# TensorE in program order in the recurrence of a fused three-stage kernel, with whole blocks of 128-row MoE1 matmuls between its steps

## The chip, the cores and the metric

The kernel runs on one core of one Trainium2 chip. The metric is the device time of one execution in microseconds (us); lower is better. A core has a matmul engine (TensorE; PE in the profile, PEld its weight loads), VectorE (DVE), ScalarE (ACT), GpSimd (POOL) and SyncE (SP), which issues all of this kernel's DMAs. Each engine works through its own instructions in the order in which they were written, and semaphores make it wait for the others.

## The reference

Three stages follow one another. The first is a recurrence over 768 time steps for 4 batches of 8 heads of width 40; the second, MoE1, is a dense layer with an ELU; the third, MoE2, mixes 8 experts with weights from an iterated normalisation.

```python
for t in range(S):                                   # recurrence, S = 768
    y[:, :, t] = einsum('bhd,bhde->bhe', r_t, state)
    Sa = einsum('bhde,bhe->bhd', state, a_t)
    state = state * w_t[:, :, None, :] - einsum('bhd,bhe->bhde', Sa, b_t) \
            + einsum('bhd,bhe->bhde', v_t, k_t)
x = y.transpose(0, 2, 1, 3).reshape(3072, 320)
h = x @ w_in                                         # MoE1: 320 -> 2048 -> 320
g = where(h > 0, h, exp(min(h, 0)) - 1)
x = g @ w_out
P = exp(logits - max)                                # MoE2: gate, 8 normalisations, 8 experts
for e in range(8):
    out += P[:, e:e+1] * (maximum(x @ w1[e], 0) @ w2[e])
```

## The kernel before

**Recurrence.** The 768 steps are cut into 24 chunks of 32. A chunk c is worked off in named steps. E1, E2 and E3 build transposes and the masked product `Am`; E3 writes `Am` to DRAM (`Ad`), and SyncE reads it back as `LT`, laid out for a triangular solve. T (`tsolve`, L377 and L384) is that solve: 62 dependent VectorE instructions, whose result goes through DRAM (`Td`) to `TT`. E4 and H1 form the right-hand side in two PSUM banks, ScalarE copies it to `RH`, H2 multiplies it by `TT`, ScalarE writes `VU`, H3 forms the state `Y` (VectorE, L454), GpSimd scales it to `Yw`, H4 transposes `Yw` to `Ss`. O1 (copies `uE`, one on ScalarE and one on VectorE, L401), O2 (masked product `Gm`) and O3 form the output, which VectorE multiplies into `xT` and SyncE stores to `yd` in DRAM. `prep` makes the decay products (two VectorE scans, `F` and `xE`). The steps of a chunk are issued in the order of the string `PLAN["order"]`; `E3+2` means E3 for chunk c+2, `O1+-1` means O1 for chunk c-1. `TT` is so needed by H2 some one and a half chunks after its E3.

**MoE1** goes by 12 blocks of 256 tokens. A block b needs the output of chunks 2b and 2b+1: `xprep` loads the two halves `yt` from `yd` (one buffer), transposes them and splits them into `X`. A block has 16 units. `m1_mm1` is the first half of a unit, eight matmuls into one PSUM tile `ph` (L536), the last with 64 rows; then ScalarE (two `m`, then `gh`), VectorE (`g`, L542) and GpSimd (`gl`) form the activation in two parts. `m1_mm2` is the second half, for the unit two before: eight matmuls (L560 to L568) that add into `a01` and `a2`, the last with 64 columns (L568). Before, `moe1` yields after every matmul; `step` counts the recurrence's own matmuls and calls `madv` after every four of them, with weights from `PLAN["wt"]`.

**Order of instructions.** A scheduler lists each engine's instructions by priority and by its own estimate of times; matmuls of several steps and units may change places on TensorE. Nothing fixes their order but data and buffers.

**MoE2** starts when MoE1 ends: 7,680 matmuls of 512 or 320 columns (L707, L747 to L749).

Of the kernel before, what the change touches and what calls it, by code (L numbers as in the profile page):

```python
# [9 lines left out]
F32 = mybir.dt.float32  # L10
# [90 lines left out]
def build(ctx, tc, r, k, v, w, a, b, w_in, w_out, wg, w1, w2, wa_d, kb_d, re_d, ro_d, vt_d, wp_d, consts, out, C, off):  # L101
# [13 lines left out]
    V, A, G, T, SY = nc.vector, nc.scalar, nc.gpsimd, nc.tensor, nc.sync  # L115

# [51 lines left out]
    # ------------------------------------------------------------ MoE1 weights  # L168
# [40 lines left out]
    # ------------------------------------------------------------ recurrence  # L209
# [101 lines left out]
    def E1(c):  # L311
        z = st[c]
        z.KB = r2.tile([128, 2, H * D], F32, tag="KB", name="KB", bufs=3)
        for u in range(2):
            for g in range(NG):
                T.transpose(PS["E1"][u][:, 128 * g:128 * g + HR], z.KE[0:HR, g, u, :], ident[0:HR, 0:HR])  # L316
                yield
            o, i = unpad(z.KB[:, u, :], PS["E1"][u])
            cp("KB", u, o, i)

    def E2(c):
# [3 lines left out]
        for g in range(NG):  # L325
            T.transpose(PS["E2"][0][:, 128 * g:128 * g + HR], xv[0:HR, g, :], ident[0:HR, 0:HR])
            yield
# [3 lines left out]
    def masked(PS, K, lhs, rhs, dst):  # L331
        for u in range(2):
            for g in range(NG):
                for bi in range(2):
                    x0 = 64 * (NG * u + g)
                    T.matmul(PS[64 * bi:64 * bi + 64, x0:x0 + 64], lhsT=lhs(u, g)[0:K, 64 * bi:64 * bi + 64], rhs=rhs[0:K, g, u, :, C * bi:C * bi + C], start=True, stop=True)  # L336
# [66 lines left out]
    def H1(c):  # L403
# [7 lines left out]
        for j in range(2):  # L411
            for g in range(NG):
                for bb in range(B):
                    T.matmul(PS["H1"][j][C * bb:C * bb + C, D * g:D * g + D], lhsT=z.aE[64 * j:64 * j + D, g, C * bb:C * bb + C], rhs=Ywv[64 * j:64 * j + D, g, bb, :], start=False, stop=True, skip_group_check=True)
                    yield
            cp("RH", j, z.RH[:, HD2 * j:HD2 * j + HD2], PS["H1"][j][:, 0:HD2])

    def H2(c):
        z = st[c]
        for h in range(H):  # L420
            for u in range(2):
                x = h % NG * 2 + h // NG
                T.matmul(PS["H2"][0][64 * u:64 * u + 64, D * x:D * x + D], lhsT=z.TT[64 * u:64 * u + 64, x, :], rhs=z.RH[64 * u:64 * u + 64, D * h:D * h + D], start=True, stop=True)
# [9 lines left out]
    def H3(c):  # L433
# [3 lines left out]
        for bi in range(2):  # L437
            for g in range(NG):
                for u in range(2):
                    for j in range(2):  # L440
# [3 lines left out]
                        T.matmul(PS["H3"][bi][64 * j:64 * j + D, c0:c0 + D], lhsT=z.KB[p0:p0 + 2 * C, u, D * h:D * h + D], rhs=z.VU[p0:p0 + 2 * C, u, D * (2 * g + j):D * (2 * g + j) + D], start=True, stop=True)  # L444
# [11 lines left out]
    def H4(c):  # L456
        if c == 0:
            return
        for i in range(2 * NG):
# [3 lines left out]
            T.transpose(PS["H4"][x][:, 128 * y:128 * y + HR], yw, ident[0:HR, 0:HR])  # L463
# [7 lines left out]
    def O1(c):  # L471
# [14 lines left out]
    def O3(c):  # L486
# [24 lines left out]
    def xprep(blk):  # L511
        X = xtiles[blk] = (late[0] if blk % 2 else mt).tile([128, 6, 256], F32R, tag=f"X{blk % 2}", name="X", bufs=1)
        for t in range(2):
# [6 lines left out]
            for i in range(3):  # L520
                T.transpose(ps[:, 128 * i:128 * i + 128], yt[:, 128 * i:128 * i + 128], ident)
# [7 lines left out]
    ORD1 = ((0, 0, 128), (1, 1, 128), (2, 2, 128), (0, 3, 128), (1, 4, 128), (3, 0, 128), (4, 1, 128), (2, 5, 64))  # L529
# [21 lines left out]
    def m1_mm2(blk, f):  # L551
# [540 lines left out]
```

## Time and profile before

| | |
|---|---|
| time, median of 3 runs | 2424.52 us (2417.68 to 2428.02) |
| span of the profiled execution | 2419.9 us (the profile gives no other time for it) |
| busy in it | PE 94%, DVE 47%, ACT 30%, POOL 20% |
| mean granted TensorE clock | 0.943 |
| first copy to `RH` of chunk 2, 5, 21, 23 | 141.6, 269.9, 881.2, 936.1 us |

The span runs from the first to the last instruction of the one execution that was profiled. A busy PE is not a PE at its peak: ends of matmuls are modelled, and a wait inside a row of matmuls counts as busy. The copies to `RH` stand once in each chunk, right behind H1, and so mark its beat; the stretches below are cut there. A granted clock of 1.00 is 2.4 GHz, 0.50 is 1.2 GHz, and a number between them is a mean over both.

### The profile page before, as it was taken

Reading aid. Unit: us, or ns where it says so; the run is one execution under the profiler, and the core shown is the slowest. Engines: PE = TensorE matmul, PEld = TensorE weight load, DVE = VectorE, ACT = ScalarE, POOL = GpSimd, SP = SyncE. Lnnn points to the kernel's source line nnn. Section 1 sums busy time; section 2 is a strip of 40 time slices with the busy share of each in tenths; the row PEclk is TensorE's granted clock in tenths of the full one; section 3 lists DMA queues with packets and bytes.
Section 4 is the critical chain, followed back from the end, with each engine's and each line's share of the span. In section 5 each row is a group of like instructions: output and inputs, shape, how many; then the busy total and the mean of one; then the engine's idle time right before and its main releaser. Section 6 shows DMA issues by size and latency. Waiting matters only on the chain.

```text
span 2419.9 us, 48157 instructions
## 1 busy us (share of the span) xinstructions
PE 2281.2 (94%) x19908; PEld 2023.0 (84%) x19908; DVE 1127.5 (47%) x2878; ACT 733.8 (30%) x1627; POOL 486.9 (20%) x570
## 2 busy tenths in 40 slices
PE   2479999999999999999999999999999999999998
PEld 2467888888888888889999999999999999999997
DVE  7898677777677874153222222222222222222222
ACT  2344344444434445532311211211212212212111
POOL 6354333333333322500200200200200101001000
PEclk8568888899899999999999999999999999999999
DMA  5343333323233332210100100100100100000000
GB/s 153 109 142 87 94 76 89 87 79 93 70 99 78 81 82 63 82 59 1 49 1 1 49 1 1 49 1 4 46 1 12 37 1 25 24 1 19 12 25 32
DMA packets 171771, 121.67 MB, mean 50 GB/s; under 512 B 103000, under 2 KB 151512, under 8 KB 171544
## 3 DMA queue, kind: packets, MB, share of 16 engines
q1 hardware_dynamic: 171544, 118.52, 17.9%
q8 instruction: 158, 2.59, 0.4%
q14 instruction: 69, 0.57, 0.1%
HBM read 99.99 MB, written 18.48 MB: 49 GB/s over the span
## 4 chain that ended last, share of the span: by engine, by line
PE 79%; DVE 12%; DMA 5%; issue 2%; SPq 1%; POOL 1%; ACT 1%; DVEq 0%; ACTq 0%
PE h L707 29%; PE pa L748 9%; PE pa L749 9%; PE pa L747 9%; PE ph L536 7%; DVE Wk L384 3%; DMA WA<-in_wa 2%; DVE Tt L377 2%; PE a L560 2%; PE a L562 2%; PE a L564 1%; DMA LT<-Ad 1%; DVE F L290 1%; DVE Am L340 1%; PE P L336 1%
## 5 line engine op out<-in xcount | busy, mean ns | idle before, releaser
L707 PE MATMUL h<-X,a 128*128 128x512 f32 x3072 | 776.5, 395 | 0.0
L711 DVE SCALAR_TENSOR_TENSOR hl<-h,hh 128x512 fp32r<-128x512 f32 x384 | 264.8, 690 | 875.6 <-ACT hh L710 875.2
L707 PEld LDWEIGHTS h<-X,a 128*128 128x128 f32 x3072 | 564.5, 188 | 103.5
L710 ACT ACTIVATE hh<-h 128x512 fp32r<-128x512 f32 x384 | 230.2, 600 | 1021.6 <-PE h L707 1018.1
L748 PE MATMUL pa<-a,hl 128*128 128x320 f32 x1536 | 474.7, 310 | 0.0
L747 PE MATMUL pa<-a,hh 128*128 128x320 f32 x1536 | 472.1, 308 | 0.3 <-ACT logits L587 0.3
L749 PE MATMUL pa<-a,hh 128*128 128x320 f32 x1536 | 468.6, 309 | 0.0
L536 PE MATMUL ph<-X,Wt 128*128 128x256 f32 (+1 forms) x1536 | 309.1, 325 | 5.1 <-DVE g L542 5.0
L748 PEld LDWEIGHTS pa<-a,hl 128*128 128x128 f32 x1536 | 288.7, 188 | 16.0
L747 PEld LDWEIGHTS pa<-a,hh 128*128 128x128 f32 x1536 | 288.8, 188 | 14.7 <-ACT logits L587 0.4
L749 PEld LDWEIGHTS pa<-a,hh 128*128 128x128 f32 x1536 | 287.3, 188 | 0.0
L675 POOL TENSOR_TENSOR a<-rw,a 128x384 fp32r<-128x384 f32 x64 | 65.1, 1016 | 1061.8 <-ACT a L673 1048.4
L536 PEld LDWEIGHTS ph<-X,Wt 128*128 128x128 f32 (+1 forms) x1536 | 237.5, 207 | 42.6 <-issue 7.4
L377 DVE TENSOR_TENSOR Tt<-Wk,LT 128x60 f32<-128x60 f32 (+24 forms) x744 | 208.7, 285 | 44.2 <-DMA LT<-Ad 25.9
L384 DVE TENSOR_TENSOR Wk<-Wk,Tt 128x60 f32<-128x60 f32 (+24 forms) x744 | 210.1, 287 | 16.6
L546 POOL TENSOR_TENSOR gl<-g,gh 128x256 fp32r<-128x256 f32 x192 | 145.8, 762 | 278.6 <-ACT gh L544 260.5
L758 DVE SCALAR_TENSOR_TENSOR acc<-pa,Pg,acc 128x320 f32<-128x320 f32 x168 | 84.3, 544 | 114.8 <-PE pa L749 114.8
L542 DVE SCALAR_TENSOR_TENSOR g<-m,ph 128x256 f32<-128x256 f32 x192 | 79.7, 416 | 123.5 <-ACT m L540 120.4
L544 ACT ACTIVATE gh<-g 128x256 fp32r<-128x256 f32 x192 | 79.2, 416 | 158.6 <-DVE g L542 59.6
L539 ACT ACTIVATE m<-ph 128x256 f32<-128x256 f32 x192 | 71.5, 381 | 120.6 <-PE ph L536 119.2
L540 ACT ACTIVATE m<-m 128x256 f32<-128x256 f32 x192 | 78.5, 417 | 4.1
L316 PE MATMUL P<-cst,KE 104*128 104x104 f32 x192 | 32.3, 300 | 46.7 <-DVE Am L340 23.5
(173 smaller groups left out, 2474.0 us busy)
## 6 DMA issues: line engine op xcount, KB each, us to landing
LT<-Ad SPq DMA_DIRECT2D x24, 512.0 KB
rw<-in_moe_w SPq DMA_DIRECT2D x64, 160.0 KB
WA<-in_wa SPq DMA_DIRECT2D x24, 416.0 KB
KE<-in_kb SPq DMA_DIRECT2D x24, 416.0 KB
rw<-in_moe_w SPq DMA_DIRECT2D x64, 128.0 KB
VU<-in_vt SPq DMA_DIRECT2D x24, 320.0 KB
raw<-in_wp SPq DMA_DIRECT2D x16, 384.0 KB
raw<-in_moe_w_out SPq DMA_DIRECT2D x16, 320.0 KB
```

Source lines behind the costliest of these rows:

```text
L377: V.tensor_tensor(out=tv, in0=Wk[:, 0:ni, j:j + 1].to_broadcast([128, ni, nt]), in1=z.LT[:, j, j + 1:C].unsqueeze(1).to_broadcast([128, ni ...
L384: dve["T"] = V.tensor_tensor(out=Wk[:, 0:ni, j + 1:C], in0=Wk[:, 0:ni, j + 1:C], in1=tv, op=ALU.subtract)
L536: T.matmul(ph, lhsT=Wt[0:kp, wi, 128 * f:128 * f + 128], rhs=X[0:kp, xi, :], start=(i == 0), stop=(i == 7))
L542: V.scalar_tensor_tensor(out=g, in0=m, scalar=-1.0, in1=ph, op0=ALU.add, op1=ALU.max)
L546: G.tensor_tensor(out=gl, in0=g, in1=gh.bitcast(F32), op=ALU.subtract)
L707: T.matmul(h, lhsT=a1[:, wi, :], rhs=X[bk][:, xi, :], start=(i == 0), stop=(i == 7))
L710: A.activation(out=hh, in_=h, func=AF.Relu)
L711: V.scalar_tensor_tensor(out=hl, in0=h, scalar=0.0, in1=hh.bitcast(F32), op0=ALU.max, op1=ALU.subtract)
L747: T.matmul(o, lhsT=hh[:, ts_], rhs=a2[:, 0, :], start=(f == 0), stop=False)
L748: T.matmul(o, lhsT=hl[:, ts_], rhs=a2[:, 0, :], start=False, stop=False)
L749: T.matmul(o, lhsT=hh[:, ts_], rhs=a2[:, 1, :], start=False, stop=(f == NF2 - 1))
L758: V.scalar_tensor_tensor(out=at, in0=o, scalar=Pg[:, tt, e:e + 1], in1=at, op0=ALU.mult, op1=ALU.add)
```

## The change

From chunk 2 on TensorE's instructions are issued in program order: every matmul and transpose of the recurrence, of `xprep`, of MoE1 and of the gate is wrapped in `pin`, which keeps it behind the one before. `moe1` yields after half a unit, so that `m+2` in the new order string issues eight matmuls of `m1_mm1` and eight of `m1_mm2` in one piece, and `m+3` three such halves. Nothing is issued inside a step any more. A chunk has 16 halves, 8 units; chunks 2 to 4 have two thirds of that. `xprep` has a place of its own, `x`. The last matmul of each half is widened: L536's eighth from 64 rows to 128 (the added rows of `Wt` meet rows of `X` that are now written too), L568's from 64 columns to 128.

```diff
-    "order": "E4 O1+-1 H1 ld+3 lu+1 m+8 O2+-1 m+4 O3+-1 H2 prep+2 H3 E3+2 T+2 E1+2 E2+2 H4 m+4 lv w",
+    "order": "E4 H1 m+2 O1+-1 H2 m+3 O2+-1 H3 m+3 ld+3 lu+1 prep+2 O3+-1 m+2 H4 E3+2 T+2 m+2 E1+2 m+2 x E2+2 m+2 lv w",
...
+    def pin(ins):
+        return tc.keep_in_program_order(ins) if chain["on"] else ins
...
-            V.tensor_tensor(out=X[0:64, 5, sl], in0=pv[0:64, 2, :], in1=X[0:64, 2, sl].bitcast(F32), op=ALU.subtract)
+            V.tensor_tensor(out=X[:, 5, sl], in0=pv[:, 2, :], in1=X[:, 2, sl].bitcast(F32), op=ALU.subtract)
...
-    ORD1 = (..., (4, 1, 128), (2, 5, 64))
+    ORD1 = (..., (4, 1, 128), (2, 5, 128))
...
-            T.matmul(ph, lhsT=Wt[0:kp, wi, 128 * f:128 * f + 128], rhs=X[0:kp, xi, :], start=(i == 0), stop=(i == 7))
-            yield
+            pin(T.matmul(ph, lhsT=Wt[0:kp, wi, 128 * f:128 * f + 128], rhs=X[0:kp, xi, :], start=(i == 0), stop=(i == 7)))
...
-        T.matmul(a2[0:64], lhsT=Wo(f)[:, 256:320], rhs=gl, start=False, stop=e, skip_group_check=True)
-        yield
+        pin(T.matmul(a2, lhsT=Wo(f)[:, 256:384], rhs=gl, start=False, stop=e, skip_group_check=True))
...
-                yield from m1_mm1(*units[i])
+                m1_mm1(*units[i])
+                yield
             if i >= LAG:
-                yield from m1_mm2(*units[i - LAG])
+                m1_mm2(*units[i - LAG])
...
+        chain["on"] = True
+        acc = 0
+        for c in range(2, NCH + 1):
             for n, o in order:
...
                 elif n == "m":
-                    madv(o)
+                    acc += o * (2 if c < 5 else 3)
+                    madv(acc // 3)
+                    acc %= 3
+                elif n == "x":
+                    try_xprep()
```

How the order moves is shown at two places; the lines of the changed kernel lie two higher in the recurrence (L414 is now L416) and one lower at the end of a unit.

First TensorE, H1 in a chunk of the middle. Before, its 32 matmuls (`P<-Yw,aE`; the profile lists each of them as two) stand in pieces between matmuls of MoE1 (`a<-gh`, `a<-gl`):

```order
L414 MATMUL P_99<-Yw,aE 32x40 x10
L560 MATMUL a_4977<-gh,WoA 128x256
L414 MATMUL P_99<-Yw,aE 32x40 x5
L414 MATMUL P_100<-Yw,aE 32x40
L562 MATMUL a_4977<-gl,WoA 128x256
L564 MATMUL a_4977<-gh,WoA 128x256
L560 MATMUL a_4977<-gh,WoA 128x256
L562 MATMUL a_4977<-gl,WoA 128x256
L564 MATMUL a_4977<-gh,WoA 128x256
L414 MATMUL P_100<-Yw,aE 32x40 x15
L568 MATMUL a_4978<-gl,WoA 64x256
```

In the changed kernel E4 (L367) and H1 (L416) stand in one piece, and a whole unit behind them:

```order
L367 MATMUL P_99<-VU,Am_118 64x40 x8
L367 MATMUL P_100<-VU,Am_118 64x40 x8
L416 MATMUL P_99<-Yw,aE 32x40 x16
L416 MATMUL P_100<-Yw,aE 32x40 x16
L538 MATMUL ph<-X,Wt 128x256 x8
L561 MATMUL a_4109<-gh,WoA 128x256
L562 MATMUL a_4109<-gl,WoA 128x256
L563 MATMUL a_4109<-gh,WoA 128x256
L561 MATMUL a_4109<-gh,WoA 128x256
L562 MATMUL a_4109<-gl,WoA 128x256
L563 MATMUL a_4109<-gh,WoA 128x256
L564 MATMUL a_4110<-gh,WoA 128x256
```

Over the whole program the runs of other matmuls between MoE1's go from 325 to 162; in the middle chunks there are seven.

Then VectorE, between the mask that ends E3 (`Am`) and the first instruction of the solve that it feeds (`Tt`, 128x31). Before:

```order
L340 TENSOR_TENSOR Am_118<-P_102,cst 64x16x32 x2
L293 RECIPROCAL dq<-F 104x16
L295 SCALAR_TENSOR_TENSOR xE<-wq,dq 104x512
L454 TENSOR_TENSOR Y<-P_99,Yw 104x8x40
L454 TENSOR_TENSOR Y<-P_100,Yw 104x8x40
L542 SCALAR_TENSOR_TENSOR g<-m,ph 128x256
L401 COPY uE<-P_102 80x512
L377 TENSOR_TENSOR Tt<-Wk,LT 128x31
```

In the changed kernel, at the same place of an odd chunk:

```order
L342 TENSOR_TENSOR Am_118<-P_102,cst 64x16x32 x2
L543 SCALAR_TENSOR_TENSOR g<-m,ph 128x256 x2
L297 SCALAR_TENSOR_TENSOR xE<-wq,dq 104x512
L543 SCALAR_TENSOR_TENSOR g<-m,ph 128x256
L379 TENSOR_TENSOR Tt<-Wk,LT 128x31
```

`Y` and `uE` have moved out of it, into the solve; in even chunks the last steps of the solve before, two `g` and two `X` stand there.

## Rows read from the trace of the kernel before

**Rows 1.** Chain that ended last, shares of the span by engine.

```profile
PE 79%; DVE 12%; DMA 5%; issue 2%; SPq 1%; POOL 1%; ACT 1%; DVEq 0%; ACTq 0%
```

**Rows 2.** Stretches: length, busy of each engine (instructions), clock, DMA share, GB/s.

```profile
core 0: us, PE busy (x) PEld busy (x) DVE busy (x) ACT busy (x) POOL busy (x), PEclk, DMA share, GB/s
141.60:269.90 128.30, 113.94 (x1511) 96.61 (x1511) 107.08 (x325) 54.72 (x144) 54.19 (x66) 0.79 0.38 101
269.90:881.20 611.30, 580.60 (x8293) 503.10 (x8280) 467.17 (x1394) 268.40 (x680) 205.76 (x240) 0.90 0.33 85
881.20:936.10 54.90, 54.90 (x951) 47.01 (x937) 35.35 (x115) 26.44 (x68) 13.92 (x19) 1.00 0.21 53
936.10:1040.00 103.90, 99.92 (x792) 87.65 (x780) 24.08 (x51) 53.94 (x132) 42.09 (x54) 0.97 0.28 82
1040.00:2419.90 1379.90, 1372.70 (x7617) 1240.75 (x7615) 373.37 (x655) 288.95 (x515) 100.25 (x106) 1.00 0.06 19
```

**Rows 3.** The same stretches, copies to RH on ScalarE alone.

```profile
269.90:881.20 611.30, 9.26 (x32) 0.90 0.33 85
```

**Rows 4.** The same stretches, matmuls and weight loads of L536 alone.

```profile
269.90:881.20 611.30, 206.79 (x1024) 157.02 (x1024) 0.90 0.33 85
881.20:936.10 54.90, 20.51 (x112) 15.54 (x112) 1.00 0.21 53
936.10:1040.00 103.90, 38.80 (x224) 31.44 (x224) 0.97 0.28 82
```

**Rows 5.** Timeline of PE: start, length, line, tiles, rows*columns, shapes, count.

```profile
616.68 0.28 PE L566 MATMUL a<-gh,WoB 128*128 128x256 f32 x1
616.79 0.28 PE L568 MATMUL a<-gl,WoB 128*64 128x256 f32 x1
616.91 0.28 PE L566 MATMUL a<-gh,WoB 128*128 128x256 f32 x1
...
617.03 0.28 PE L568 MATMUL a<-gl,WoB 128*64 128x256 f32 x1
617.24 1.13 PE L423 MATMUL P<-RH,TT 64*64 64x40 f32 x32
618.29 1.72 PE L536 MATMUL ph<-X,Wt 128*128 128x256 f32 x9
```

**Rows 6.** Timeline of PE around a matmul of 64 rows.

```profile
975.79 0.28 PE L566 MATMUL a<-gh,WoB 128*128 128x256 f32 x1
976.00 0.38 PE L536 MATMUL ph<-X,Wt 64*128 64x256 f32 x1
976.31 1.43 PE L707 MATMUL h<-X,a 128*128 128x512 f32 x5
```

**Rows 7.** Timeline of PE, a piece of H1 between MoE1 matmuls.

```profile
611.89 0.99 PE L536 MATMUL ph<-X,Wt 128*128 128x256 f32 x7
612.81 0.35 PE L414 MATMUL P<-Yw,aE 40*32 40x40 f32 x22
613.09 1.41 PE L536 MATMUL ph<-X,Wt 128*128 128x256 f32 x8
```

**Rows 8.** Timeline of DVE, from Am to the solve's first step, in two chunks.

```profile
777.31 1.40 DVE L340 TENSOR_TENSOR Am<-P,cst 64x512 f32<-64x512 f32 x2
...
787.77 1.40 DVE L377 TENSOR_TENSOR Tt<-Wk,LT 128x31 f32<-128x31 f32 x1 [0.97 <-DMA LT<-Ad]
...
816.48 1.38 DVE L340 TENSOR_TENSOR Am<-P,cst 64x512 f32<-64x512 f32 x2
...
818.28 1.22 DVE L295 TENSOR_TENSOR_SCAN xE<-wq,dq 104x512 f32<-104x512 f32 x1
...
820.68 0.18 DVE L384 TENSOR_TENSOR Wk<-Wk,Tt 128x8 f32<-128x8 f32 x1
821.29 0.42 DVE L542 SCALAR_TENSOR_TENSOR g<-m,ph 128x256 f32<-128x256 f32 x1 [0.43 <-ACT m L540]
823.81 0.69 DVE L401 COPY uE<-P 80x512 f32<-80x512 f32 x1 [2.11 <-PE P L477]
825.59 0.30 DVE L377 TENSOR_TENSOR Tt<-Wk,LT 128x31 f32<-128x31 f32 x1 [1.09 <-DMA LT<-Ad]
```

**Rows 9.** Waits between 269.9 and 881.2 us: in total, times, longest.

```profile
DVE g L542 <- ACT m L540: 49.2, 40, 4.1
...
DVE Tt L377 <- DMA LT<-Ad: 23.4, 12, 4.4
...
PE P L316 <- DVE Am L340: 19.0, 13, 2.3
...
DVE wr L287 <- DMA WA<-in_wa: 9.3, 12, 1.8
```

**Rows 10.** Timeline of SyncE, then of PE: a load of yt and its transposes.

```profile
959.96 0.32 SPq L518 DMA_DIRECT2D yt<-yd  x1
...
962.27 0.52 PE L521 MATMUL P<-cst,yt 128*128 128x128 f32 x3 [1.05 <-DMA yt<-yd]
```

More of the change, by code (lines that the diff above doesn't have):

```diff
@@ L335, in masked @@
                     x0 = 64 * (NG * u + g)
-                    T.matmul(PS[64 * bi:64 * bi + 64, x0:x0 + 64], lhsT=lhs(u, g)[0:K, 64 * bi:64 * bi + 64], rhs=rhs[0:K, g, u, :, C * bi:C * bi + C], start=True, stop=True)
+                    pin(T.matmul(PS[64 * bi:64 * bi + 64, x0:x0 + 64], lhsT=lhs(u, g)[0:K, 64 * bi:64 * bi + 64], rhs=rhs[0:K, g, u, :, C * bi:C * bi + C], start=True, stop=True))
                     yield
@@ L422, in H2 @@
                 x = h % NG * 2 + h // NG
-                T.matmul(PS["H2"][0][64 * u:64 * u + 64, D * x:D * x + D], lhsT=z.TT[64 * u:64 * u + 64, x, :], rhs=z.RH[64 * u:64 * u + 64, D * h:D * h + D], start=True, stop=True)
+                pin(T.matmul(PS["H2"][0][64 * u:64 * u + 64, D * x:D * x + D], lhsT=z.TT[64 * u:64 * u + 64, x, :], rhs=z.RH[64 * u:64 * u + 64, D * h:D * h + D], start=True, stop=True))
                 yield
@@ L499, in O3 @@
                 for u in range(2):
-                    T.matmul(PO[j][64 * u:64 * u + 64, D * g:D * g + D], lhsT=Gm[:, u, 2 * g + j, :], rhs=z.KB[:, u, D * h:D * h + D], start=(c == 0 and g == 0), stop=True, skip_group_check=True)
+                    pin(T.matmul(PO[j][64 * u:64 * u + 64, D * g:D * g + D], lhsT=Gm[:, u, 2 * g + j, :], rhs=z.KB[:, u, D * h:D * h + D], start=(c == 0 and g == 0), stop=True, skip_group_check=True))
                     yield
@@ L585, in gate @@
                 kp = 128 if kk < 2 else 64
[L586 removed]
+                pin(T.matmul(ps[:, NE * i:NE * i + NE], lhsT=x2[0:kp, kk, 128 * i:128 * i + 128], rhs=wgs[0:kp, kk, :], start=(kk == 0), stop=(kk == 2)))
         A.copy(out=logits[:, 2 * blk:2 * blk + 2, :], in_=ps[:, 0:2 * NE].rearrange("p (t e) -> p t e", t=2))
@@ L959, in try_xprep, with ready @@
         def try_xprep():
-            bk, f = divmod(ms["n"], NF1)
+            bk = ms["n"] // NF1
             xp = ms["xp"]
-            if (late or xp == 0) and xp < NB1 and (xp <= bk or (xp == bk + 1 and f >= 6)) and ("O3", 2 * xp + 1) in done:
+            if (late or xp == 0) and xp < NB1 and xp <= bk + 1 and ("O3", 2 * xp + 1) in done:
                 xprep(xp)
                 ms["xp"] += 1
+        def ready(n):
+            blk = min(n // NF1, NB1 - 1)
+            if blk >= ms["xp"]:
+                return False
+            if not wgen:
+                return True
+            return all(("i", f) in cvd for f in range(min(n + 1, NF1))) and all(("o", f) in cvd for f in range(max(0, min(n - LAG + 1, NF1))))
         def msteps():
@@ L969, in msteps @@
                     try_xprep()
-                while min(ms["n"] // NF1, NB1 - 1) >= ms["xp"] or (wgen and not (all(("i", f) in cvd for f in range(min(ms["n"] + 1, NF1))) and all(("o", f) in cvd for f in range(max(0, min(ms["n"] - LAG + 1, NF1)))))):
+                while not ready(ms["n"]):
                     yield
@@ L987, in build, with madv, step @@
         done = {("ld", 0), ("ld", 1)}
-        acc_ = [0.0]
-        def madv(r):
-            acc_[0] += r
-            if acc_[0] >= 1:
-                with tc.high_priority(offset=PLAN["mo"]) if PLAN["mo"] else ExitStack():
-                    while acc_[0] >= 1:
-                        next(mg)
-                        acc_[0] -= 1
-        def step(n, c, rate):
+        def madv(n):
+            with tc.high_priority(offset=PLAN["mo"]):
+                for _ in range(n):
+                    next(mg)
+        def step(n, c):
             if 0 <= c < NCH and (n, c) not in done:
-                try_xprep()
                 po = PLAN["po"].get(n, 0)
                 with tc.high_priority(offset=po) if po else ExitStack():
-                    g_ = fns[n](c)
-                    if g_ is not None:
-                        k_ = 0
-                        for _ in g_:
-                            k_ += 1
-                            if k_ == PLAN["grp"]:
-                                madv(rate * PLAN["wt"].get(n, 1) * k_)
-                                k_ = 0
+                    run_all(fns[n](c) or ())
                 done.add((n, c))
@@ L1040, in build @@
                 else:
-                    step("T" if n == "t" else n, cs[0], 0)
-        for c in range(-4, NCH + 1):
+                    step("T" if n == "t" else n, cs[0])
+        chain["on"] = True
+        acc = 0
+        for c in range(2, NCH + 1):
             for n, o in order:
@@ L1046, in build @@
                 elif n == "m":
-                    madv(o)
+                    acc += o * (2 if c < 5 else 3)
+                    madv(acc // 3)
+                    acc %= 3
+                elif n == "x":
+                    try_xprep()
                 else:
-                    step(n, c + o, PLAN["rate"])
+                    step(n, c + o)
             st.pop(c - 2, None)
+        chain["on"] = False
         ms["free"] = True
```

39 lines of the change are left out of this document (15 added, 24 removed), and 2 rows, old and new, of the table PLAN.

## The prediction

> **What bounds the kernel now.** I start with the chain that ended last: TensorE holds 79% of it and VectorE 12% [rows 1]. A share over the whole span says little here, so next I cut the span at the copies to `RH`, which mark a chunk [rows 2]. Of 2,419.9 us, the 1,379.9 from 1,040 us on are MoE2, with TensorE busy 1,372.7 of them; the change leaves MoE2 as it is. The stretch that it works on is 141.6 to 936.1 us, chunks 2 to 22. Its middle, 269.9 to 881.2 us, has 32 copies to `RH`, two a chunk, so 16 chunks [rows 3], of 611.3 / 16 = 38.2 us each. In such a chunk TensorE is busy 580.6 / 16 = 36.3 us, VectorE 467.2 / 16 = 29.2, ScalarE 16.8, GpSimd 12.9, and 1,024 / 8 / 16 = 8 units of MoE1 are done [rows 2 to 4]. TensorE bounds the chunk. But VectorE comes second with 29.2, and it can't reach full use: the reader is to look at how its 9.0 idle us arise [rows 8, 9]. Between the mask `Am` and the first step of the solve lies the way of `Am` through DRAM to `LT`, 7.7 us in one chunk and 9.1 in another [rows 8], and VectorE can only fill it with what stands there in its own order.
>
> **What TensorE saves.** Three things, from single rows.
>
> 1. *The 64-row matmul.* Matmuls of 128 rows follow each other after 0.12 us [rows 5]. The 64-row one starts 0.21 us after its predecessor and its successor 0.31 us after it [rows 6]. Two such steps cost 0.52 instead of 0.24, so 0.28 us a unit, 8 x 0.28 = 2.3 us a chunk. Widening it costs nothing visible, for the moving side stays at 256 columns.
> 2. *The 64-column matmul* (L568) starts 0.11 us after its predecessor and is followed after 0.12 [rows 5]. Widening it gains nothing.
> 3. *Fewer pieces.* Where MoE1 gives way to H2 the step is 0.21 instead of 0.12 us [rows 5]. For a piece of H1 it is similar: seven L536 from 611.89 to 612.81 us are 0.92 where seven steps of 0.12 are 0.84, and the 22 small matmuls take 0.28 [rows 7], of which I put 0.12 on the way back (between nothing and those 0.28). A piece so costs about 0.21. The order has 325 - 162 = 163 pieces less in 22 chunks, 7.4 a chunk: 1.6 us (0.7 to 2.7 by those ends).
>
> On the second the Trainium skill weighs otherwise: TensorEngine Tiling, section Key Properties, says that a change of tiling mode drains the engine. The row of L568 shows no such drain between 128 and 64 columns; by the page the second widening would save about as much as the first, some 8 us in the 28 units behind chunk 23, and the forecast would lie that much lower. The measured row decides.
>
> So 36.3 - 2.3 - 1.6 = 32.4 us. The clock was 0.90 in that stretch [rows 2], between levels of 0.5 and 1 a fifth of the time at half; that fifth, 7.6 us, would be 3.8 at full speed. TensorE's work in a chunk is then 28.6 us at a clock of 1.00 and 32.4 at 0.90. A check: the two chunks from 881.2 to 936.1 us at clock 1.00, without idle time, took 27.5 us each, with 7 units and less recurrence work [rows 2, 4].
>
> **What takes its place: VectorE.** Its work is the same, 29.2 us a chunk: the one widened instruction (`X`) has 128 columns as before, and I cost it at nothing (its whole length is some 0.3 us in two chunks, as an estimate from the rows of its neighbours). Its idle time is where the new order matters. Of the 9.0 us, 49.2 / 16 = 3.1 are `g` waiting for ScalarE and through it for MoE1's matmuls, 1.5 `LT`, 0.6 `WA` [rows 9], the rest waits for TensorE as that of 2.11 us for `uE` [rows 8]. With TensorE ahead, waits for it go. The way through DRAM stays: from `Am` to the solve's first step 7.7 to 9.1 us, mean 8.4 [rows 8]. In the new order an odd chunk has three `g` and `xE` there, 3 x 0.42 + 1.22 = 2.5 us; an even one the last steps of the solve before (0.2 us each, some eight), two `g` and two `X`, 3.3 us as an estimate from the same rows. `Y` and `uE`, 2 us of work that stood there, are now inside the solve. Left idle are 5.9 and 5.1 us, 5.5 on average, and 0.6 for `WA`: 29.2 + 5.5 + 0.6 = **35.3 us a chunk**. This is above 28.6 and above 32.4, so VectorE decides, and of the 5.8 us or more that TensorE gains 2.9 come through.
>
> **Queued behind the waits.** In program order whatever TensorE waits for holds MoE1 up too. Two waits are new in kind. E1's second half writes the bank that the mask `Am` reads; it waited 13 times, 19.0 us in all, before [rows 9]. Now VectorE reaches `Am` some 5 us after TensorE could go on, so each E1 waits, and E2, three units, E4 and H1 behind it. That is VectorE's lead, already in the 35.3. And `xprep`'s second half can't load before its first is transposed, for `yt` has one buffer: 2.3 us from issue to use [rows 10], every other chunk; it stands behind `Td` and `LT` in SyncE's queue. TensorE has 35.3 - 28.6 = 6.7 us to spare, so I cost it at nothing; if TensorE were the bound it would be 1.2 us a chunk, 18 in all.
>
> **The sum.** Middle: 16 x (38.2 - 35.3) = -46 us. Chunks 2 to 4: VectorE is busy 107.1 of 128.3 us [rows 2], idle 7.1 a chunk against 6.1: -3. Chunks 21 and 22: TensorE is the bound, 14 units lose their 0.28 (-4), some two more units at 16 x 0.12 = 1.9 come in (+4): 0. Behind chunk 23: the new order has done 16 + 8 x 18 = 160 units when H1 of chunk 23 ends and leaves 32; before, 224 / 8 = 28 were left [rows 4]. That is 4 x 1.9 = +8 and 28 x 0.28 = -8: 0. In all -49, a span of 2,419.9 - 49 = 2,371. The median of the runs lies 4.6 above the profiled span, so **2,376 us**. By the spread of the `LT` way (7.7 to 9.1, 0.7 to each side) it is 2,376 +/- 11; with half of the vanished 2.9 us still waited for, 2,399; with the 5.5 us filled by half, 2,332. Its own range is 2,332 to 2,400. The ends of TensorE's 1.6 us don't enter, as long as VectorE decides.
>
> **The rivals.**
>
> *VectorE doesn't wait* (chance 0.10). If `LT` came back within the work that stands there, a chunk would be VectorE's 29.2 us (TensorE's 28.6 is close): 16 x 9.0 = -144, with the -3, 2,277 us. For it: TensorE has the room. Against it: even the faster of the two `LT` ways is 7.7 us, and only 2.5 to 3.3 us of work stand in it [rows 8].
>
> *The wait only changes its place* (0.13). VectorE idles 9.0 us a chunk as before, since every engine is in fixed order and each `g` stands in front of steps of the solve: a `g` whose matmuls are held up holds the solve up. A chunk then stays at 38.2, and with -3 the time is 2,421 us. For it: `g` is the largest wait of VectorE now [rows 9]. Against: units now come in whole blocks, evenly.
>
> *The clock falls* (0.07), the one on the other side. The clock is 1.00 where TensorE never idles and 0.79 where it is idle 11% of the time [rows 2]. TensorE now has to stand still some 5 us a chunk before E1, and if it then works on at half speed, its 28.6 us grow by each us that it does so. It decides from 35.3 / 28.6 on, when 23% of its work runs at 1.2 GHz, and the kernel gets slower than before at 34%. With half of the work at half speed a chunk takes 42.9 us: 16 x 4.7 = +75, with the -3 2,497 us. Against: a unit in one piece is 1.9 us of dense matmuls, and 16 halves are spread over the chunk.
> The Trainium skill has this as a rule, TensorE: Matmul & The Clock Gate, section Why this matters for your kernels: gaps between bursts of matmuls bring the lower clock back. The rows at 0.79, 0.90 and 1.00 agree with it; how long TensorE stays low in the new order no run here shows yet.
>
> **How the numbers follow.** The forecast has 0.70, the rivals 0.10, 0.13 and 0.07. About 0.5%, 12 us, is what a measurement of this kernel can tell from no change: 2,412 to 2,437 us. The forecast lies below 2,412 but for 0.02, the first rival too, the second inside but for 0.03, the third beyond 2,437: faster 0.80, same 0.13, slower 0.07. The range leaves out half of the first rival and of the third and parts of the edges: 2,330 to 2,422.
>
> **What the changed profile would show.** Right: the middle chunks 35 us apart, VectorE busy 29 of them and idle 5 to 6 between `Am` and the solve's first step, waiting for `LT`; E1 waiting for `Am` in every chunk; no step of 0.31 us behind L538's eighth matmul; a clock of 0.9 or more. Wrong, if the first step of the solve no longer waits for `LT` (first rival), if `g` is still VectorE's largest wait (second), or if TensorE is busy throughout at a clock under 0.8 (third). If H2 waits for `TT`, or the second load of `yt` holds TensorE up by much more than 2.3 us, there is a wait that this sum misses.

## The result and the profile after

The changed kernel takes 2,436.21 us (median of 4 runs, 2,433.81 to 2,439.20), the kernel before on the same chip 2,423.99. The ratio is 1.0057, with a 95% interval of 1.0035 to 1.0078: slower by 0.6%, where 2% faster was forecast. The profiled execution has a span of 2,431.9 us against 2,419.9.

The page first: TensorE's busy time and the chain that ended last, which answers to [rows 1].

```profile
PE 2185.4 (90%) x19908; PEld 1991.4 (82%) x19908; DVE 1127.6 (46%) x2878; ACT 731.1 (30%) x1627; POOL 503.8 (21%) x570
PE 67%; DVE 19%; DMA 8%; issue 2%; SPq 2%; POOL 1%; ACT 1%; DVEq 0%; ACTq 0%; POOLq 0%
```

TensorE is busy 96 us less than before (2,281.2 on the page of before) and the kernel is no faster. The chain has lost twelve hundredths of TensorE and got seven of VectorE and three of DMA in their place. Where that happens is seen in the stretches cut at the copies to `RH`, as in [rows 2]: chunks 2 to 4, the middle (16 chunks), chunks 21 and 22; then two single chunks of the middle.

```profile
137.10:258.90 121.80, 78.47 (x1242) 72.97 (x1245) 103.44 (x295) 48.73 (x121) 54.00 (x64) 0.85 0.38 98
258.90:876.40 617.50, 517.20 (x8301) 479.41 (x8288) 463.35 (x1392) 263.37 (x681) 220.44 (x240) 0.90 0.32 84
876.40:944.30 67.90, 60.41 (x1006) 57.44 (x995) 41.55 (x143) 29.39 (x76) 16.57 (x21) 0.90 0.20 52
...
723.50:754.10 30.60, 30.14 (x545) 27.93 (x535) 23.39 (x69) 16.57 (x44) 9.81 (x12) 1.00 0.31 82
754.10:799.30 45.20, 33.04 (x533) 30.34 (x524) 33.42 (x105) 16.31 (x42) 16.93 (x19) 0.85 0.34 88
```

Against [rows 2] the middle grew by 617.5 - 611.3 = 6.2 us and chunks 21 and 22 by 13.0; chunks 2 to 4 shrank by 6.5; the time ahead of chunk 2 by 4.5; and all that lies behind chunk 22 grew from 1,483.8 to 1,487.6, by 3.8. The sum is +12.0. In the middle TensorE is busy 517.2 / 16 = 32.3 us a chunk instead of 36.3, so its saving is there; but it now stands idle 6.3 us a chunk instead of 1.9. And the chunks differ: of the 16, those without `xprep` take 31 to 33 us (two early ones 38), those with it 43 to 46 (the two next to those 40 to 41). Most of the first kind lie below the forecast 35.3, all of the second well above it. In the chunk of 754.1 us TensorE is idle for 12.2 us: 4.8 are a stop of the kind shown next, 3.6 a wait for `gl`, 2.1 one for `Am`.

What TensorE does in such a chunk (timeline of PE; in brackets the idle time ahead and what ended it):

```profile
634.28 0.49 PE L523 MATMUL P<-cst,yt 128*128 128x128 f32 x3
640.29 0.88 PE L523 MATMUL P<-cst,yt 128*128 128x128 f32 x3 [5.52 <-DMA yt<-yd]
640.96 0.90 PE L328 MATMUL P<-cst,xE 104*128 104x104 f32 x4
641.55 2.06 PE L538 MATMUL ph<-X,Wt 128*128 128x256 f32 x8
643.41 0.41 PE L561 MATMUL a<-gh,WoB 128*128 128x256 f32 x1
643.62 0.41 PE L562 MATMUL a<-gl,WoB 128*128 128x256 f32 x1
...
645.24 1.66 PE L367 MATMUL P<-VU,Am 128*64 128x40 f32 x32
646.83 0.79 PE L416 MATMUL P<-Yw,aE 40*32 40x40 f32 x64
```

The same time as stretches, with the granted clock: the load of the second half, the work up to E4, and what follows it from H1 on.

```profile
635.75:640.29 4.54, 0.00 (x0) 0.03 (x1) 1.01 (x3) 0.00 (x0) 2.14 (x2) 0.92 0.76 205
640.30:645.20 4.90, 4.90 (x23) 4.72 (x23) 4.52 (x16) 1.72 (x4) 0.85 (x2) 0.50 0.31 57
646.80:650.00 3.20, 3.20 (x88) 3.12 (x85) 2.92 (x9) 1.76 (x5) 1.44 (x2) 1.00 0.02 5
```

And SyncE's queue ahead of that load:

```profile
634.49 0.56 SPq L359 DMA_DIRECT2D LT<-Ad  x1
635.11 0.59 SPq L390 DMA_DIRECT2D Td<-Wk  x1
635.75 0.60 SPq L520 DMA_DIRECT2D yt<-yd  x1
```

TensorE has transposed the first half of `yt` by 634.8. Only then can the second load be issued; it goes out at 635.75, behind `LT` and a `Td`, and its data is used 4.5 us later, at 640.29. TensorE stands for 5.5 us with E2, a unit, E4 and H1 queued behind the transposes, and afterwards works at a granted clock of 0.50 (1.2 GHz) for 4.9 us: L561 to L562 is 0.21 us, where such a step takes 0.12 in [rows 5]. H1, which starts the next chunk, comes at 646.83.

The other seven stops of the middle are alike: the load goes out 0.0 to 1.6 us after the first half's transposes and 1.3 to 1.6 us behind an `LT`, and takes 3.5 to 4.9 us from issue to use, with the DMA engines busy for 0.71 to 0.82 of that time. Where TensorE waited for a load of `yt` with no `LT` shortly before it, the load took 2.3 us [rows 10] and, three times in run e5 below, 2.4 to 2.5, at a DMA share of 0.45 to 0.51. In the changed kernel the stop in chunk 22, with three `Td` ahead, had 2.8 us from issue to use, the one before chunk 5, with `KE` (416 KB) and four `Ad` ahead, 3.7. One of the three of e5:

```profile
719.51:722.00 2.49, 2.25 (x21) 2.08 (x19) 0.52 (x2) 1.62 (x5) 1.16 (x2) 1.00 0.45 103
```

That `LT` makes the load longer is read from these rows; no run took `LT` alone away from there. The waits of the whole middle (engine, line, what it waited for; us in total, times, longest) answer to [rows 9]:

```profile
PEld P L523 <- issue: 40.6, 8, 5.9
ACT X L526 <- PE P L523: 39.6, 15, 5.8
...
PE P L523 <- DMA yt<-yd: 29.8, 6, 5.7
PE a L562 <- POOL gl L547: 25.6, 8, 6.1
PE P L318 <- DVE Am L342: 16.3, 8, 2.1
PE P L523 <- DVE Tt L379: 8.6, 2, 4.8
...
DVE Tt L379 <- DMA LT<-Ad: 52.5, 13, 8.3
DVE g L543 <- ACT m L541: 38.5, 35, 2.2
```

Each of the eight `xprep` of the middle stops TensorE: as its weight load shows it, for 40.6 / 8 = 5.1 us. ScalarE waits as long for the same transposes, with `gh` behind them, and the waits for `gl` are new. VectorE's wait for `g` has gone from 49.2 to 38.5 only, that for `LT` has grown from 23.4 to 52.5.

### The profile page after: what moved, and what is told of

It reads as the page before. It is cut to its first block, busy times and chain, and to the rows that moved or that the text cites. A ratio compares the mean times of both kernels' runs of the same rounds, so it can differ in the third digit from the quotient of the medians.

```text
span 2431.9 us, 47949 instructions
## 1 busy us (share of the span) xinstructions
PE 2185.4 (90%) x19908; PEld 1991.4 (82%) x19908; DVE 1127.6 (46%) x2878; ACT 731.1 (30%) x1627; POOL 503.8 (21%) x570
## 4 chain that ended last, share of the span: by engine, by line
PE 67%; DVE 19%; DMA 8%; issue 2%; SPq 2%; POOL 1%; ACT 1%; DVEq 0%; ACTq 0%; POOLq 0%
PE h L704 29%; PE pa L746 9%; PE pa L745 9%; PE pa L744 9%; DVE Wk L386 5%; DVE Tt L379 5%; PE ph L538 3%; DMA WA<-in_wa 2%; DMA LT<-Ad 1%; DVE g L543 1%; DMA yt<-yd 1%; DVE F L292 1%; DVE Gm L342 1%; DVE Am L342 1%; PE a L561 1%
## 5 line engine op out<-in xcount | busy, mean ns | idle before, releaser
L538 PE MATMUL ph<-X,Wt 128*128 128x256 f32 x1536 | 252.2, 311 | 5.2 <-DVE g L543 5.1
L547 POOL TENSOR_TENSOR gl<-g,gh 128x256 fp32r<-128x256 f32 x192 | 159.1, 830 | 389.2 <-ACT gh L545 280.3
L538 PEld LDWEIGHTS ph<-X,Wt 128*128 128x128 f32 x1536 | 216.6, 209 | 14.3 <-DVE g L543 8.5
L386 DVE TENSOR_TENSOR Wk<-Wk,Tt 128x60 f32<-128x60 f32 (+24 forms) x744 | 215.2, 292 | 17.9
L425 PE MATMUL P<-RH,TT 64*64 64x40 f32 x768 | 33.7, 248 | 48.7 <-DMA TT<-Td 47.1
```

What stands on the lines that cost most here:

```text
L386: dve["T"] = V.tensor_tensor(out=Wk[:, 0:ni, j + 1:C], in0=Wk[:, 0:ni, j + 1:C], in1=tv, op=ALU.subtract)
L538: pin(T.matmul(ph, lhsT=Wt[0:kp, wi, 128 * f:128 * f + 128], rhs=X[0:kp, xi, :], start=(i == 0), stop=(i == 7)))
L547: G.tensor_tensor(out=gl, in0=g, in1=gh.bitcast(F32), op=ALU.subtract)
```

## The experiments

Each time is a median, beside the kernel before on the same chip; the chunk is the mean of chunks 5 to 20 in one profiled execution. Executions of one kernel lie up to 15 us apart (e3: 2,476 to 2,490), so a few tenths of a us in the last column decide nothing.

| Kernel | us | ratio to before (95%) | us a chunk |
|---|---|---|---|
| changed kernel | 2,436.2 | 1.0057 (1.0035 to 1.0078) | 38.6 |
| e1: second buffer for `yt` | 2,400.7 | 0.9888 (0.9846 to 0.9931) | 37.0 |
| e2: before, with the widenings alone | 2,402.6 | 0.9893 (0.9847 to 0.9939) | 37.5 |
| e3: changed kernel, free order | 2,483.2 | 1.0225 (1.0178 to 1.0271) | 42.1 |
| e4: changed kernel, not widened | 2,462.7 | 1.0146 (1.0105 to 1.0187) | 39.1 |
| e5: `xprep` in two halves | 2,393.0 | 0.9866 (0.9838 to 0.9894) | 36.8 |
| e6: e1, `LT`'s way on ScalarE's queue | 2,460.2 | 1.0153 (1.0119 to 1.0187) | 40.6 |
| e7: e1, half of the solve | 2,373.1 | 0.9789 (0.9762 to 0.9816) | 36.3 |
| e8: e1, full rate from chunk 2 | 2,423.0 | 0.9983 (0.9966 to 1.0000) | 38.6 |
| e9: e5, mm2 three units behind | 2,401.6 | 0.9896 (0.9870 to 0.9922) | 37.8 |
| e10: e5, two units ahead of E1 | 2,396.4 | 0.9884 (0.9862 to 0.9905) | 37.2 |
| e11: e9 and e10 | 2,426.8 | 0.9998 (0.9981 to 1.0014) | 39.1 |
| e12: e5, `xprep` between H2 and O2 | 2,392.1 | 0.9873 (0.9834 to 0.9912) | 36.4 |
| e13: e12 and e10 | 2,396.3 | 0.9882 (0.9840 to 0.9923) | 36.5 |
| e14: e5, half of mm1 | 2,400.9 | 0.9896 (0.9865 to 0.9927) | 37.4 |
| e16: e5, half of the solve | 2,362.3 | 0.9737 (0.9708 to 0.9766) | 36.5 |
| e15: e5, both halves left out | 2,305.5 | 0.9503 (0.9470 to 0.9536) | 33.0 |

The first theory was that the second load of `yt` is the missed wait (A). Its rivals: waits in a fixed order only change their place (B), and VectorE with the way of `LT` sets the pace (C).

**e1, the suspected wait alone taken away.**

```diff
-                yt = mt.tile([128, 384], F32, tag="yt", name="yt", bufs=1)
+                yt = (late[0] if t else mt).tile([128, 384], F32, tag=f"y{t}t" if t else "yt", name="yt", bufs=1)
```

> The changed kernel with a second buffer for yt, so that the load for the second half of xprep is issued before TensorE needs it; all else stays in program order. Theory A (the second load of yt is the missed wait: in the changed kernel TensorE stands 5 to 6 us before the second three transposes of xprep, every other chunk, with units, E4 and H1 queued behind it): the chunks with xprep fall from 45 to about 38 us, the others stay at 32 or rise a little, some 7 us x 8 in the middle and as much in one more block, 2,370 to 2,395 us. Theory B (the waits only change places: with a fixed order TensorE stops at the next late input instead, gl, g or Am): at most 2 us a block come back, 2,418 to 2,440. Theory C (VectorE and the way of LT through DRAM set 38.6 us a chunk): no change, 2,425 to 2,440, and the chunks become even, 38 and 38.

35 us come back: 2,400.7 lies between the two ranges, 6 us above A's and 17 below B's. The waits of the middle:

```profile
DVE Tt L379 <- DMA LT<-Ad: 62.7, 15, 6.4
DVE g L543 <- ACT m L541: 25.0, 21, 2.2
...
PE P L318 <- DVE Am L342: 20.1, 10, 2.3
PE ph L538 <- DVE g L543: 15.7, 15, 2.8
PE a L562 <- POOL gl L547: 13.2, 8, 2.8
PE P L523 <- ACT gh L545: 10.3, 8, 1.3
```

No wait for `yt` is left there, but part of it has come out as waits for `Am`, `g` and `gh`, and VectorE waits longer for `LT`. So A names the cause, and B says why 35 us came back and not the 41 to 66 that A had.

**e2 to e4, the change taken apart.** e2 is the kernel before with the three widened instructions; e4 is the changed kernel with the three narrow again. e3 drops the program order:

```diff
     def pin(ins):
-        return tc.keep_in_program_order(ins) if chain["on"] else ins
+        return ins
```

> The kernel before with the three widenings alone (a 128-row matmul in place of the 64-row one, a2 at 128 columns, X of 128 partitions), scheduler's order and small pieces as before. If TensorE decides the chunk, 8 units x 0.28 = 2.3 us a chunk come back in 16 chunks and 0.28 in each of the other 60 or so units: 2,424 - 37 - 17 = 2,370 us. If VectorE with the way of LT decides from about 35.3 us on, it stops at -2.3 a chunk as well and gives the same: 2,370 to 2,385. If neither is true and VectorE's waits set the pace of 38.2 us, 2,405 to 2,424.

> The changed kernel without the fixed program order on TensorE: same list of steps, whole blocks of eight matmuls, same widenings, but TensorE's instructions go where the scheduler puts them. Theory A and theory B both say that the fixed order is what stands in the way (matmuls that could run wait behind one whose input is late): 2,370 to 2,400 us. Theory C, or that the new list of steps is what is bad: 2,420 to 2,440.

> The changed kernel with the three widenings undone, program order kept: 0.28 us more TensorE time a unit. If TensorE's stops and its work add up (theories A and B: behind each stop it is TensorE that sets the pace), all 192 units pay, 2,436 + 54 = 2,490 us, or at least 2,465. If VectorE decides the chunk (theory C), only the units outside the middle pay, 2,436 + 17 = 2,453 or less.

The middle of e2:

```profile
273.00:872.50 599.50, 543.49 (x8257) 493.01 (x8246) 461.41 (x1375) 265.26 (x680) 205.07 (x240) 0.91 0.34 87
```

Widening is worth 20 us on the kernel before and 26 on the changed one. TensorE's work falls as forecast, from 36.3 to 543.5 / 16 = 34.0 us a chunk, by 2.3; but the chunk loses only 0.7 us (38.2 to 37.5), and 0.5 on the changed kernel (39.1 to 38.6): 11.8 and 8.0 us in the middle, the rest outside it. TensorE's work alone, then, was not what bounded the chunk, before or after. e2 lies 2 us below the range of its third case, VectorE's waits, and far above the other two; e4 lies between its two. e3 is slower than either of its ranges and speaks against A and B as they were put: the fixed order is not what makes the kernel slow; without it the same list of steps is 47 us slower still. Its middle:

```profile
252.00:925.00 673.00, 623.80 (x8266) 539.02 (x8266) 449.54 (x1380) 269.67 (x678) 206.85 (x239) 0.86 0.30 77
```

TensorE is busy 39.0 us a chunk for the work that takes 32.3 in program order; a part of that is the clock, 0.86 against 0.90. Counted in the rows, MoE1's matmuls stand in some 23 groups a chunk there, in 15.4 in the kernel before and in 7.0 in the changed one.

**e5, another way to take the wait away**: the halves of `xprep` at the same place of two chunks that follow each other, with one buffer.

```diff
-    def xprep(blk):
-        X = xtiles[blk] = (late[0] if blk % 2 else mt).tile([128, 6, 256], F32R, tag=f"X{blk % 2}", name="X", bufs=1)
-        for t in range(2):
+    def xprep(blk, t):
+        if t == 0:
+            xtiles[blk] = (late[0] if blk % 2 else mt).tile([128, 6, 256], F32R, tag=f"X{blk % 2}", name="X", bufs=1)
+        X = xtiles[blk]
+        if True:
...
-            if (late or xp == 0) and xp < NB1 and xp <= bk + 1 and ("O3", 2 * xp + 1) in done:
-                xprep(xp)
+            if (late or xp == 0) and xp < NB1 and xp <= bk + 1 and ("O3", ms["xp"]) in done:
+                xprep(xp, ms["xp"] % 2)
```

> The changed kernel with xprep cut in two: its halves, one load of yt and three transposes each, stand at the same place in two chunks that follow each other, so that one buffer is enough; program order kept. With the second buffer alone 35 us came back, and the chunks stayed uneven (33 and 41 us, with 7 and 9 units). Theory A (the load of yt was the wait, and what stays uneven is the work itself): even chunks of 37 us, 2,395 to 2,405. Theory D (what is left hangs on two waits for ScalarE within one xprep, 5 us in one chunk and none in the next): 35 us a chunk, 2,370 to 2,390.

2,393.0 us, 43 less than the changed kernel, between A's range and D's; with e12 the fastest that computes everything, 1.3% ahead of the kernel before. Of the 41.0 us between the profiled spans 617.5 - 588.1 = 29.4 lie in the middle, 3.7 for each of the eight stops of 5.1; the rest lies in chunks 2 to 4 (6.4), 21 and 22 (3.6) and behind them. The chunk is 36.8, not 35.

**e6 and e7, VectorE's share.** e6 issues `Ad` and `LT` from ScalarE's queue (`SY.dma_start` becomes `A.dma_start` in both places); e7 shortens the solve:

```diff
-        for j in range(C - 1):
+        for j in range(C // 2):
```

> Second buffer for yt, and the way of Am through DRAM to LT (four stores Ad, the load LT) issued from ScalarE's queue in place of SyncE's, where every other chunk the four Ad stand behind three Td and the load of KE, 3 us later than in the chunks between. Theory E (VectorE's wait for LT, 62.7 us in 16 chunks, is what keeps the chunk at 37.0): half of those 3 us a chunk come back, 2,372 to 2,390. Rival (ScalarE now holds copies and gh back while LT waits for Ad to land): 2,400 to 2,430.

> Second buffer for yt, and 15 of the 31 steps of each solve left out, so that the output is not the reference's: VectorE has about 7 us less work a chunk, TensorE the same. Theory E (VectorE with its wait for LT decides): the chunk falls from 37.0 by 5 us or so to TensorE's 31 to 32, 2,300 to 2,330 us. Theory F (TensorE's own order with its late inputs decides): 2,385 to 2,402.

In e6 the wait for `LT` does fall, to a third; but ScalarE holds back what others need, and the kernel loses 60 us against e1, 30 more than the rival's range allows. The waits of VectorE between 262 and 910 us:

```profile
DVE g L543 <- ACT m L541: 40.0, 12, 9.7
DVE X L527 <- ACT X L526: 33.3, 5, 8.6
DVE Tt L379 <- DMA LT<-Ad: 19.7, 9, 4.0
```

In e7 VectorE is busy 343.2 / 16 = 21.5 us a chunk instead of 28.5, and the chunk falls by 0.7. The time falls by 28 us, between the two ranges, but only 592.2 - 580.5 = 11.7 of that lie in the middle. VectorE alone does not set the pace.

**e8, more units early.** The line that takes two thirds of the rate below chunk 5 takes it whole.

```diff
-                    acc += o * (2 if c < 5 else 3)
+                    acc += o * 3
```

> Second buffer for yt, and the full rate of 8 units from chunk 2 on in place of 5.3 in chunks 2 to 4: 8 units move from behind chunk 23 into chunks 2 to 4, where TensorE is busy 76 of 117 us and waits 29.8 for TT. If they fill these waits: 8 x 1.9 = 15 us less, 2,386. If they stand in front of what the recurrence waits for or behind H2's wait for TT: chunks 2 to 4 grow by as much, 2,397 to 2,405.

It gave neither: 22 us slower than e1. Chunks 2 to 4 take 118.5 us instead of 117.0, so nothing is filled, and the middle is back at 38.6, though `yt` has its two buffers. TensorE's longest wait there:

```profile
PE ph L538 <- DVE X L527: 34.6, 8, 5.3
```

MoE1, further ahead, starts each new block right behind `xprep` and waits for its `X`, 4.3 us eight times: the same chain, one link later.

**e9 to e13, the next waits one by one.** These are TensorE's largest waits in the middle of e5:

```profile
PE P L318 <- DVE Am L342: 22.6, 12, 3.2
...
PE a L564 <- POOL gl L549: 20.7, 11, 5.3
```

e9 sets `LAG = 3` with a third buffer for `gh` and `gl`, which every third unit of a block takes; the order of steps changes in e10 and e12 (e11 is e9 and e10, e13 is e12 and e10):

```diff
-m+2 H4 E3+2 T+2 m+2 E1+2 m+2 x E2+2 m+2 lv w
+m+2 H4 E3+2 T+2 m+4 E1+2 x E2+2 m+2 lv w
...
-H2 m+3 O2+-1 ... E1+2 m+2 x E2+2 m+2
+H2 m+3 x O2+-1 ... E1+2 m+2 E2+2 m+2
```

> The split xprep, and mm2 of a unit three units behind its mm1 in place of two, with a third buffer for gh and gl: TensorE's waits for gl (20.7 us in 16 chunks) go. Theory F (each wait of TensorE in its fixed order adds to the chunk): 20 us less, 2,365 to 2,380. Theory E (VectorE with LT decides): 2,388 to 2,398.

> The split xprep, and the two units that stood behind E1 now ahead of it, so that TensorE has 3.8 us more to do before it needs what VectorE's mask frees: the waits of E1 for Am (22.6 us in 16 chunks) go. Theory F: 15 to 22 us less, 2,370 to 2,380. Theory E: no change, 2,388 to 2,398, with more waits for gl, since four units now stand together.

> Both of these edits together on the split xprep. Theory F: the sum of both, 2,350 to 2,360. Theory E: 2,385 to 2,398.

> The split xprep with its three transposes moved from between E1 and E2 to between H2 and O2, half a chunk later than yt is stored and at a time when the bank that they share with E1 and the mask is free. Theory G (what keeps the chunk at 36.8 us is the chain mask Am, E1, its copy, xprep, E2, xE, which all pass through one bank and through VectorE): with xprep out of it the chunk falls by 1 to 2 us, 2,365 to 2,380. Theory H (a wait removed there only comes out at the next late input): 2,388 to 2,400. If units now wait for X, as they did at the full rate, 2,400 to 2,425.

> The same, with the two units that stood behind E1 ahead of it: E1 no longer waits for Am and there is no transpose of xprep behind E1 that waits for its copy. Theory G: the 31.7 us of that wait and the 32.8 us of xE's for E2 go, 2,350 to 2,370. Theory H: 2,388 to 2,400.

No edit brought its waits back as time; e10, e12 and e13 stay within 4 us of e5, e9 loses 9, and e11, which no theory has, 34. In e10 the two waits are gone, and this stands in their place:

```profile
PE P L525 <- ACT KB L403: 31.7, 16, 3.0
...
PE a L564 <- POOL gl L549: 2.5, 8, 0.5
PE P L318 <- DVE Am L342: 1.4, 4, 0.4
```

In e13, where `xprep` no longer stands behind E1, TensorE waits for the solve:

```profile
PE P L425 <- DMA TT<-Td: 37.3, 24, 4.4
```

e12's middle is the shortest of these, 36.4, but only by 0.3. So theories F and G fall, and H holds for these: from one order to the next a wait only comes out elsewhere. (Theory E has e10's time in its range too; e7 and e16 speak against it.) In e9 TensorE waits 18.0 us, once in each block, for the VectorE instruction that frees `a2` at the block's end (6.1 in e5), in e11 23.1 us for the ScalarE copy that frees `a01`. Whether these waits are all that makes the two slower, no run shows.

**e14 to e16, which engine sets what is left.** e14 leaves out four of eight mm1 matmuls within the stretch in program order, e16 half of the solve as e7 did, e15 both, all on e5.

```diff
-        for i, (wi, xi, kp) in enumerate(ORD1):
+        order1 = ORD1[:4] if chain["on"] else ORD1
+        for i, (wi, xi, kp) in enumerate(order1):
```

> The split xprep, and within the stretch in program order four of a unit's eight mm1 matmuls left out, so that the output is not the reference's: TensorE has 8 x 4 x 0.12 = 3.8 us less work a chunk, the rest is the same. Theory T (TensorE's work and its waits add up, about 32 + 5 us): the chunk falls from 36.8 to 33 us. Theory V (VectorE with its waits decides): it stays at 36 to 37. If both are close together, about half comes through, 35.

> The split xprep and 15 of the 31 steps of each solve left out, so that the output is not the reference's: VectorE has 7 us less work a chunk. On the kernel with two buffers of yt this gave 36.3 in place of 37.0 us a chunk. Theory T: 36 us again. Theory V: 32 or less.

> Both left out, 3.8 us of TensorE's and 7 us of VectorE's work a chunk. Theory T: 33 us as with the matmuls alone. Theory V: 32 or less, as with the solve alone. If the two stand close together or wait in turn for each other, more than the sum of the two comes back, 31 us or less.

The middle of e5, then of e14, e16 and e15 (columns as in [rows 2]):

```profile
253.20:841.30 588.10, 506.14 (x8299) 469.10 (x8287) 453.87 (x1387) 258.20 (x680) 222.26 (x242) 0.93 0.35 89
```

```profile
255.60:853.50 597.90, 467.36 (x7782) 434.12 (x7770) 459.73 (x1384) 265.94 (x680) 214.21 (x240) 0.85 0.35 87
```

```profile
229.80:813.60 583.80, 508.21 (x8316) 474.21 (x8304) 346.73 (x909) 260.68 (x681) 217.90 (x242) 0.92 0.36 90
```

```profile
232.00:759.90 527.90, 462.40 (x7782) 425.50 (x7771) 319.39 (x904) 265.24 (x681) 212.94 (x239) 0.88 0.39 98
```

36.8, 37.4, 36.5, 33.0 us a chunk: less work on TensorE alone gives nothing back, as theory V has it, less on VectorE alone 0.3, as theory T has it, and less on both 3.8. The 0.3 and the rise to 37.4 are within what single executions differ by; the 3.8 are not. Neither theory can have both; the third case, the two close together, has the sign, but not the sizes: it had 35 for e14 and 31 for e15. In e14 the clock falls from 0.93 to 0.85, and TensorE is busy for only 2.4 us a chunk less instead of 3.8. What each waits for, between 255 and 820 us: TensorE in e14, then VectorE in e16 (in e5's middle these are 10.1 and 28.1 us):

```profile
PE P L425 <- DMA TT<-Td: 65.6, 11, 10.0
```

```profile
DVE g L545 <- ACT m L543: 73.4, 48, 2.6
```

With less of its own work TensorE waits for the solve, and VectorE for what TensorE feeds it. Neither cut alone moves the chunk by more than 0.6 us from 36.8. One caution on e16: a part of the old stop is back in it, some 1.1 us a chunk, so its 0.3 may be less than VectorE's work is worth there:

```profile
PE P L525 <- DMA yt<-yd: 17.0, 11, 2.9
```

## Why the prediction was wrong

**The step that failed** is the one on `xprep`'s second load: "TensorE has 35.3 - 28.6 = 6.7 us to spare, so I cost it at nothing". Both halves of it are off. The stop is not 2.3 us but 5.1: the load goes out late and takes 3.5 to 4.9 us behind `LT` and `Td`, where the text itself had put it without pricing that. And TensorE did not have the 6.7 us to spare: 28.6 us was its work at full clock and without a wait, while in e5, without the stop, it is busy for 31.6 us of a chunk and waits for 5.1; in e16, with 6.7 us less work on VectorE, a chunk still takes 36.5 us. Ten blocks have this stop, one in chunks 2 to 4, eight in the middle and one in chunk 22: 10 x 5.1 = 51 us, of which e5 got 43 back and e1 35. The condition at the end of the prediction, that the load holds TensorE up by much more than 2.3 us, is what came true; "if TensorE were the bound it would be 1.2 us a chunk" was the case to take, with the larger price.

**TensorE's saving** was right: 32.3 us busy a chunk at clock 0.90, forecast 32.4 at 0.90. Its two terms hold one by one: the widenings alone take 2.3 us a chunk (e2, 34.0 us), and from e2 to the changed kernel, with the fewer pieces, it is another 1.6. The step of 0.31 us behind the narrow matmul is gone. The second widening gained nothing, as its row had it: in the changed kernel too L565 follows L564 after 0.12 us and is followed after 0.12 (starts at 629.58, 629.70 and 629.82 us). That speaks for the row and against the drain that the Trainium skill states (TensorEngine Tiling (Array Packing), section Key Properties), as far as 128 to 64 columns goes; no run widened that one alone.

**VectorE's 35.3 us** was mis-sized. Its work is right, 463.4 / 16 = 29.0 against 29.2. Its idle time is 154.2 / 16 = 9.6 us a chunk in the changed kernel and 8.4 in e5, not 6.1. `LT` takes less of it than I had put, 52.5 / 16 = 3.3 and not 5.5; but the waits for `g`, which I had let go with TensorE ahead, stay at 38.5 / 16 = 2.4. TensorE is not ahead: it waits for `Am` at E1 (16.3 us, in 8 of the 16 chunks, where the forecast had every one) and for `gl` (25.6). That its next unit, whose `g` VectorE needs, is late by what it waited is argued from the order, not shown by a run. Without the `yt` wait the sum would have been 1.5 us a chunk too low, 23 us in all.

**The rivals.** *The wait only changes its place* came nearest with 2,421 us, in part by luck: its chunk of 38.2 us is close to the measured 38.6, but that holds the stop for `yt`, which this rival does not have. e9 to e13 show it at work on what is left: there the chunk of 36.4 us or more does not hang on one wait. *VectorE doesn't wait* is out (52.5 us for `LT`). *The clock falls* is out as the cause: 0.90 in the middle, as before. It adds to a stop, since the matmuls behind the one shown run at 0.50, 0.21 us apart. The rule that gaps between bursts bring the lower clock back (the Trainium skill, TensorE: Matmul & The Clock Gate, section Why this matters for your kernels) agrees with that row and with e14's 0.85. But the idle share alone does not order the clocks here: 0.90 with 5% idle time in the kernel before, 0.90 with 16% in the changed one, 0.93 with 14% in e5.

**The other terms.** Chunks 2 to 4: -6.5 for a forecast of -3. Chunks 21 and 22: +13.0 for 0. They do 16 units instead of 14, as said; but TensorE also stands idle 67.9 - 60.4 = 7.5 us there at clock 0.90, where before it had no idle time. 4.9 of these are the stop of the tenth block. In e5, without that stop, it is still +9.4, with a wait of 4.4 us for `RH` that no run followed. Behind them: +3.8 for 0. There the eleventh block's second transposes stop TensorE for 4.8 us, where the kernel before waited 1.0; but this is another stop, since e1, with two buffers, keeps it at 4.8. The transposes follow right behind the VectorE instruction that ends `X` of the first half, which has two instructions of MoE2 ahead of it.

**What stays open**: why 36.5 us a chunk is reached from both sides. That the engines hold each other is shown (e14 to e16); which link of `Am`, `LT`, the solve, `TT` and `g` would have to be shorter is not, since each wait that was taken away alone came out elsewhere. How much of the chunk the two ways through DRAM (`LT` and `TT`) hold, no run settles: e6 shortened the wait for `LT`, but made VectorE wait for ScalarE instead.

## What to carry to other kernels

Before TensorE is put in program order, list each instruction in that order whose input is loaded into a single buffer that the order itself has just emptied: its whole time from issue to use, with what stands ahead of it in the DMA queue, is paid by all that stands behind it. An engine's room to spare is its pace with its own waits at the clock that it gets, not its work at full clock; two engines that feed each other can both be idle, as in e5 for 14 and 23% of a chunk, and neither have room. When taking a wait away gives nothing, take work from both engines at once: here only that showed that the two hold each other.

## What the runs showed of the hardware

- A load of `yt` (192 KB) took 2.3 to 2.5 us from issue to use with the DMA engines busy for 0.45 to 0.51 of that time (four loads), and 3.5 to 4.9 us issued 1.3 to 1.6 us behind `LT`'s 512 KB, at 0.71 to 0.82 (eight loads).
- Behind the 5.5 us stop TensorE ran at a granted clock of 0.50 for 4.9 us (matmuls 0.21 us apart), and at 1.00 again from H1 on.
- The same TensorE work of a chunk took 39.0 us busy in some 23 groups at clock 0.86, and 32.3 in 7.0 groups at 0.90.
- Eight matmuls of 64 rows a chunk, widened to 128, took 2.3 us off TensorE's busy time (e2 against the kernel before).
